# Gated linear attention and a SoLU feed-forward block: every operation in a new written order

## The chip, the cores and the metric

The kernel runs on one core of one Trainium2 chip. The metric is the device time of one execution in microseconds (us), as a median of several runs. The core has five engines with a queue each: TensorE (PE in the profile; PEld are its weight loads), VectorE (DVE), ScalarE (ACT), GpSimd (POOL) and SyncE (SP), which here only issues DMAs. Each queue is worked off in the order in which it is written; an instruction that waits holds up all that stands behind it on its engine.

## What is computed

First a linear attention with a complex decay per key channel (batch 4, 8 heads, 768 steps, head dimension 48), then a feed-forward block over the 3072 rows of 384 numbers:

```python
mag = np.sqrt(a_re * a_re + a_im * a_im)
scale = np.minimum(mag, 0.999) / (mag + 1e-06)
...
for t in range(S):
    new_re = ar * S_re - ai * S_im          # ar, ai: a_re, a_im times scale, at step t
    new_im = ar * S_im + ai * S_re
    S_re, S_im = new_re + k_t (outer) v_t, new_im
    y[t] = q_t @ S_re
...
h = x @ w_in                                # 384 -> 1024, x: y of all heads side by side
solu = h * softmax(h)
ln = (solu - mean) / sqrt(var + 1e-06) * g_ln
out = ln @ w_out                            # 1024 -> 384
```

The weights arrive as 64-bit floats, which no engine computes with; the kernel takes their words apart and puts 32-bit floats together.

## The kernel before

The sequence is cut into six chunks of 128 steps. One unit of work, called a chunk below, is 128 steps of one of the four batch entries with all eight heads: 24 chunks, numbered c = 0 to 23. Two neighbouring chunks are a group (g = 0 to 11) and share their preparation.

*Preparation of a group* (`prep_steps`): from a_re and a_im (tiles `f_ar`, `f_ai`, 128 x 768) the logarithm of the decay and the angle per step. It is a chain of rows of VectorE and ScalarE in turn: clamp (L670, L672), `inverse` (logarithm and exponential), `s1` and `tangent`, `square`, `s2`, `s3`, `s4`. TensorE then sums the logarithms over the steps of the chunk with a triangular matrix (`totals`, tile `f_L`, L713) and the angles likewise (`phases`, tile `f_phase`, L766). Exponentials of the sums give `f_ar` and `f_ai` anew (`decay`), sines give the tile `f_cs` (`trig`). ScalarE needs one function table for exponentials and one for sines; `to_trig` and `to_exp` load them. From one chunk of a batch entry to the next the angle is carried on (`on`, L756) and so is the decay at the last step (`ends`, `tots`); both pass through a small DMA.

*Turning* (`doubled`, `turn`): k and q are scaled by the decay (`decayed`, L727), multiplied by cosine and sine (L794, tiles `f_k2`, `f_q2`, printed as `f_k` and `f_q` in the profile), and transposed by TensorE in halves of four heads (L806, `f_turned`); ScalarE copies the result out of PSUM to `f_kT` and `f_qT`.

*Attention of a chunk* (`chunk_steps`): scores (L827, tile `f_score`) and their mask (L829), the values (L843, L846, tile `f_y`) and their copy `f_xn` (L849), and the carried state (L858, `f_d`). V is also loaded a second time with its rows in reversed blocks (`f_vr`, eight small DMAs a group).

*Feed-forward of a chunk* (`ffn_steps`): transpose of x (`f_xt`, L876), up projection in two halves (`f_h`, L884), exponential and product (L892, L893, tile `f_z`), transposes of z (`f_zt`, L901) and their copies (L902), the mean and variance (`norm`, L914 and on), down projection in two halves (`f_o`, L926), and the scaling by the row's norm `f_rs` with the store (L931, L933).

*Weights* (`weight_steps`): 14 pieces, 6 of w_in and 8 of w_out. A piece is fetched to one of six `f_raw` buffers, two rows of ScalarE (`raised`, L626, L628) and three of VectorE (`convert`, L634, L636, L638) make floats of it. The eight `mean` matmuls (L650) and eight `centre` rows (L655) take the mean out of w_out, so that the layer norm's mean need not be subtracted later. From the fifth chunk on all pieces are fetched once more and inspected (L641).

The PSUM banks: two buffers `f_ps_t` that all transposes and sums take in turn, one bank for each half of the scores, one shared by values and state, two for `f_h`, one for `f_o` (which `f_mean` uses before).

The order of the rows of TensorE, VectorE and ScalarE is the order of the calls in `whole`: a written list for chunks 0 and 1, then a loop over n = 2 to 25 whose body does chunk n's attention, chunk n-1's up projection and chunk n-2's down projection with pieces of the preparation of the next groups, the even n one share, the odd n another. The rows of SP and GpSimd are put in order by the framework's scheduler. Several calls issue rows on two or three engines at once, such as `phases` with six rows on three engines.

## Time and profile before

| | |
|---|---|
| median of 3 runs | 547.28 us (545.79 to 548.36) |
| profiled execution: time, span | 545.41 us, 543.6 us |
| TensorE busy | 472.0 us, 87% |
| VectorE busy | 368.1 us, 68% |
| ScalarE busy | 305.7 us, 56% |
| moved by DMA | 44.7 MB |

The span runs from the first to the last instruction. A row of the 40 slices gives an engine's busy share in tenths for each fortieth of the span, 13.6 us. In the views of waits a row reads: who waited, `<-` for whom, us in total, how often, the longest. In the views of groups a row ends with busy us and the mean ns of one, then the idle time ahead of these rows and who ended it. In the timeline a row begins with its start and its duration in us; in brackets stands the idle time of its engine before it. A matmul of 32-bit floats is two instructions, so that x6 in the profile are three matmuls of the code.

### The profile page before, as it was taken

Reading aid. Unit: us, or ns where it says so; the run is one execution under the profiler, and the core shown is the slowest. Engines: PE = TensorE matmul, PEld = TensorE weight load, DVE = VectorE, ACT = ScalarE, POOL = GpSimd, SP = SyncE. Lnnn points to the kernel's source line nnn. Section 1 sums busy time; section 2 is a strip of 40 time slices with the busy share of each in tenths; the row PEclk is TensorE's granted clock in tenths of the full one; section 3 lists DMA queues with packets and bytes.
Section 4 is the critical chain, followed back from the end, with each engine's and each line's share of the span. In section 5 each row is a group of like instructions: output and inputs, shape, how many; then the busy total and the mean of one; then the engine's idle time right before and its main releaser. Section 6 shows DMA issues by size and latency. Waiting matters only on the chain. (4 is left out here: it accounts for less than half of the span.)

```text
span 543.6 us, 15486 instructions
## 1 busy us (share of the span) xinstructions
PE 472.0 (87%) x6756; PEld 293.1 (54%) x6756; DVE 368.1 (68%) x716; ACT 305.7 (56%) x497; POOL 17.9 (3%) x52
## 2 busy tenths in 40 slices
PE   0264745699999999999999999999999999999994
PEld 0143323455665665666666656556566656666652
DVE  5677435957777867859759669669578677564323
ACT  4766447376666566575575665665656665742220
POOL 0000000000000000000000000000000000000000
PEclk9997786899999999999999999999999999999999
DMA  9895976322624615517317305316223000000001
GB/s 210 203 245 115 183 116 191 102 57 58 120 60 69 139 45 89 119 46 128 80 47 146 60 24 110 60 32 119 45 56 80 16 3 17 16 16 2 16 16 36
DMA packets 148076, 44.74 MB, mean 82 GB/s; under 512 B 141216, under 2 KB 144288, under 8 KB 148000
## 3 DMA queue, kind: packets, MB, share of 16 engines
q1 hardware_dynamic: 147152, 43.28, 37.6%
q8 instruction: 55, 0.90, 0.7%
q10 hardware_dynamic: 848, 0.40, 0.3%
q14 instruction: 21, 0.17, 0.1%
HBM read 38.87 MB, written 4.72 MB: 80 GB/s over the span
## 5 line engine op out<-in xcount | busy, mean ns | idle before, releaser
L884 PE MATMUL f_h<-f_w_in,f_xT 128*128 128x512 f32 x288 | 135.3, 607 | 8.5 <-ACT f_xT L879 8.5
L926 PE MATMUL f_o<-f_w_out,f_zT 128*128 128x384 f32 x384 | 133.5, 492 | 2.9 <-DVE f_w_out L655 2.9
L926 PEld LDWEIGHTS f_o<-f_w_out,f_zT 128*128 128x128 f32 x384 | 70.3, 192 | 43.4 <-DVE f_w_out L655 3.1
L884 PEld LDWEIGHTS f_h<-f_w_in,f_xT 128*128 128x128 f32 x288 | 51.8, 192 | 58.5 <-issue 48.0
L892 ACT ACTIVATE f_z<-f_h 128x512 f32<-128x512 f32 x48 | 28.7, 597 | 87.9 <-PE f_h L884 87.7
L893 DVE TENSOR_TENSOR f_z<-f_h,f_z 128x512 f32<-128x512 f32 x48 | 33.1, 690 | 44.0 <-ACT f_z L892 44.0
L806 PE MATMUL f_turned<-f_mats,f_k 128*96 128x128 f32 x192 | 32.1, 293 | 17.8 <-DVE f_k L794 17.8
L902 ACT COPY f_zT<-f_zt 128x512 f32<-128x512 f32 x48 | 26.7, 587 | 25.8 <-PE f_zt L901 25.2
L806 PEld LDWEIGHTS f_turned<-f_mats,f_k 128*96 128x96 f32 x192 | 21.8, 132 | 34.8 <-DVE f_k L794 25.4
L849 DVE COPY f_xn<-f_y 128x384 f32<-128x384 f32 x24 | 13.2, 552 | 37.7 <-PE f_y L846 32.3
L808 ACT COPY f_kT<-f_turned 96x512 f32<-96x512 f32 x48 | 27.7, 576 | 18.4 <-PE f_turned L806 18.4
L713 PE MATMUL f_L<-f_lr,f_mats 128*128 128x384 f32 x48 | 19.0, 522 | 18.5 <-DVE f_lr L706 18.5
L806 PE MATMUL f_turned<-f_mats,f_q 128*96 128x128 f32 x192 | 31.1, 288 | 2.7 <-DVE f_q L794 2.7
L827 PEld LDWEIGHTS f_score<-f_qT,f_kT 96*32 96x32 f32 x1536 | 28.8, 110 | 8.0 <-issue 8.0
L829 DVE TENSOR_TENSOR f_att<-f_score,f_mats 128x512 f32<-128x512 f32 x48 | 30.8, 683 | 2.5 <-PE f_score L827 2.5
L827 PE MATMUL f_score<-f_qT,f_kT 96*32 96x96 f32 (+3 forms) x1536 | 32.0, 235 | 0.0
L714 DVE TENSOR_SCALAR f_lr<-f_L 128x384 f32<-128x384 f32 x24 | 13.3, 557 | 25.8 <-PE f_L L713 25.0
L914 DVE BATCH_NORM_STATS2 f_bs<-f_z 128x6 f32<-128x512 f32 x48 | 30.7, 681 | 0.0
L846 PE MATMUL f_y<-f_state,f_qT 96*32 96x48 f32 x1280 | 30.1, 205 | 0.0
L808 ACT COPY f_qT<-f_turned 96x512 f32<-96x512 f32 x48 | 28.1, 586 | 2.7 <-PE f_turned L806 1.5
L901 PEld LDWEIGHTS f_zt<-f_mats,f_z 128*128 128x128 f32 x192 | 21.5, 141 | 13.2 <-DVE f_lr L714 8.5
L901 PE MATMUL f_zt<-f_mats,f_z 128*128 128x128 f32 x192 | 27.9, 279 | 0.2
(101 smaller groups left out, 751.7 us busy)
## 6 DMA issues: line engine op xcount, KB each, us to landing
f_raw<-in_moe_w_in_dram SPq DMA_DIRECT2D x12, 512.0 KB, 5.7
f_raw<-in_moe_w_out_dram SPq DMA_DIRECT2D x16, 384.0 KB, 4.2
f_ar<-in_a_re_dram SPq DMA_DIRECT2D x24, 192.0 KB, 3.8
f_ai<-in_a_im_dram SPq DMA_DIRECT2D x24, 192.0 KB, 4.1
f_q<-in_q_dram SPq DMA_DIRECT2D x24, 192.0 KB, 4.3
f_k<-in_k_dram SPq DMA_DIRECT2D x24, 192.0 KB, 4.1
f_v<-in_v_dram SPq DMA_DIRECT2D x24, 192.0 KB, 4.8
out_dram<-f_ot SPq DMA_DIRECT2D x24, 192.0 KB, 1.9
```

Source lines behind the costliest of these rows:

```text
L806: nc.tensor.transpose(out=ps[0:D2, i], in_=T[nm + "2", c][:, half * 4 + i].rearrange("p u d -> p (u d)"), identity=ident)
L808: nc.scalar.copy(out=T[nm + "T", c][:, half * 512:half * 512 + 512], in_=ps[0:D2].rearrange("p i t -> p (i t)"))
L827: nc.tensor.matmul(out=ps[r0:r0 + 32, i, r:], lhsT=KT[:, x * P + r:x * P + r + 32], rhs=QT[:, x * P + r:(x + 1) * P], start=True, stop=True)
L829: nc.vector.tensor_tensor(out=st["att"][:, half * 4:half * 4 + 4].rearrange("p (i u) t -> p i u t", u=2), in0=ps.rearrange("p (i u) t -> p ...
L846: nc.tensor.matmul(out=y[r:r + 32, hs], lhsT=T["qT", c][:, x * P + r:x * P + r + 32], rhs=state[b][:, hs], start=False, stop=True)
L884: nc.tensor.matmul(out=h, lhsT=st["xT"][:, c * P:(c + 1) * P], rhs=w_in[:, c, half * 512:(half + 1) * 512], start=(c == 0), stop=(c == KD ...
L892: nc.scalar.activation(out=z, in_=h, func=AF.Exp, accum_out=sums[:, ti * B + b, half:half + 1])
L893: nc.vector.tensor_tensor(out=z, in0=h, in1=z, op=OP.mult)
L901: nc.tensor.transpose(out=ps[:, i * P:(i + 1) * P], in_=st["z"][:, c * P:(c + 1) * P], identity=ident)
L902: nc.scalar.copy(out=st["zT"][:, half * 512:(half + 1) * 512], in_=ps)
L914: nc.vector.bn_stats(out=bs[:, i], in_=z[:, i * 512:(i + 1) * 512])
L926: nc.tensor.matmul(out=st["o"], lhsT=st["zT"][:, c * P:(c + 1) * P], rhs=w_out[:, c], start=(c == 0), stop=(c == KF - 1))
```

## The change

Every call is split so that it issues rows on one engine only: `phases` becomes `phase0`, `phase1`, `nearest0`, `nearest1`, `part0`, `part1`; `score` leaves its mask to `mask`; `turn` leaves its copy to `turned`; and so on. The steps are kept in a table by name and number, and three lists of words give the order: START for the first chunks, 190 steps one by one, and EVEN and ODD for the loop, which together are one pair of chunk periods. In a word such as `kt1:2` stand the step and the chunk; in EVEN and ODD the number is added to n, and with a g it is added to the group's number. The scheduler no longer orders SP and GpSimd: their rows too come in the order of the lists. Besides, the scaling by `f_rs` moves from VectorE to ScalarE, the two small DMAs from ScalarE's queue to SP's, the verdict's rows (a check over all chunks) go to the very end, and the fetches for the inspection are at other places.

```diff
+START = """
+load_ar:0 load_ai:0 fetch:0 fetch:1 fetch:4 fetch:3 clamp:0 inverse:0 fetch:2 ratio:0 raised:0 load_ar:1
...
+EVEN = """
+turn_x:-1 solu1:-2 score0:0 zt1:-2 down0:-2 clamp:g1 load_k:g1 inverse:g1 turned_x:-1 kt1:0 ks1:g0 zT1:-2 add:-1
...
+ODD = """
+inspect:-9 qt0:1 qT0:1 zT0:-1 down1:-2 load_ar:g2 exp1:-1 scale:-2 store:-2
...
-            nc.scalar.dma_start(out=st["ends"], in_=up[P - 1:P, :])
+            nc.sync.dma_start(out=st["ends"], in_=st["ar"][P - 1:P, :])
...
-                nc.scalar.activation(out=t, in_=ps, func=AF.Identity, bias=magic)
-                nc.vector.scalar_tensor_tensor(out=t, in0=t, scalar=MAGIC, in1=ps, op0=OP.subtract, op1=OP.subtract)
+        def nearest(i):
+            nc.scalar.activation(out=st["f"][:, i * DM:(i + 1) * DM], in_=st["phase", i], func=AF.Identity, bias=magic)
...
-            nc.vector.tensor_scalar(out=o, in0=st["o"], scalar1=st["rs"], scalar2=None, op0=OP.mult)
+        def scale():
+            st["out"] = ffp.tile([P, DM], FP, tag="ot", name="f_ot")
+            nc.scalar.activation(out=st["out"], in_=st["o"], func=AF.Copy, scale=st["rs"])
...
+    for s in START.split():
+        nm, i = s.split(":")
+        go(nm, int(i))
+    for n in range(2, NC * B + 2):
+        for s in (ODD if n % 2 else EVEN).split():
+            nm, i = s.split(":")
+            go(nm, n // GB + int(i[1:]) if i[0] == "g" else n + int(i))
+    go("verdict", 0)
...
-        inner.enter_context(tc.manual_schedule(engines={mybir.EngineType.Activation, mybir.EngineType.PE, mybir.EngineType.DVE}))
+        inner.enter_context(tc.manual_schedule(engines={mybir.EngineType.Activation, mybir.EngineType.PE, mybir.EngineType.DVE,
+                                                    mybir.EngineType.SP, mybir.EngineType.Pool}))
```

Three places show what that does to the queues. The first is the start of SP's queue, the loads of the opening. Before:

```order
L592 DMA f_ai<-in_a_im_dram 128x8x48 x2
L619 DMA f_raw<-in_moe_w_in_dram 128x1024 x2
L592 DMA f_q<-in_q_dram 128x8x48 x2
L592 DMA f_k<-in_k_dram 128x8x48 x2
L619 DMA f_raw<-in_moe_w_in_dram 128x1024 x4
L592 DMA f_v<-in_v_dram 128x8x48 x2
L601 DMA f_vr<-in_v_dram 32x4x48 x8
L592 DMA f_ar<-in_a_re_dram 128x8x48 x2
L592 DMA f_ai<-in_a_im_dram 128x8x48 x2
L987 DMA f_g_ln<-in_moe_g_ln_dram 128x8x1
L619 DMA f_raw<-in_moe_w_out_dram 128x768 x5
```

and now, with `f_ends` the decay's last step, which waits for ScalarE:

```order
L626 DMA f_ai<-in_a_im_dram 128x8x48 x2
L657 DMA f_raw<-in_moe_w_in_dram 128x1024 x5
L626 DMA f_ar<-in_a_re_dram 128x8x48 x2
L626 DMA f_q<-in_q_dram 128x8x48 x2
L657 DMA f_raw<-in_moe_w_in_dram 128x1024
L626 DMA f_ai<-in_a_im_dram 128x8x48 x2
L767 DMA f_ends<-f_ar 16x1x48
L657 DMA f_raw<-in_moe_w_out_dram 128x768
L626 DMA f_k<-in_k_dram 128x8x48 x2
L657 DMA f_raw<-in_moe_w_out_dram 128x768
L826 DMA f_on<-f_f 1x16x48
L626 DMA f_v<-in_v_dram 128x8x48 x2
```

The weights of w_in and the second group's a_re have moved ahead of the first group's k and v, and the two small DMAs stand between the loads. The second place is VectorE's queue at the end of the second group's preparation, from the last row of its phases to the doubled k and q of chunk 2. Before:

```order
L769 TENSOR_SCALAR f_cs_650<-f_f_651 128x8x48
L634 TENSOR_SCALAR f_w_out_121<-f_raw_314 128x384
L636 SCALAR_TENSOR_TENSOR f_w_out_121<-f_raw_314,f_w_out_121 128x384
L638 ISA f_w_out_121<-f_w_out_121,f_bits_671 128x768
L727 TENSOR_TENSOR f_k_325<-f_k_325,f_ai_182 128x384
L727 TENSOR_TENSOR f_q_322<-f_q_322,f_ar_179 128x384
L794 TENSOR_TENSOR f_k2_679<-f_cs_650,f_k_325 128x768
L794 TENSOR_TENSOR f_q2_681<-f_cs_650,f_q_322 128x768
```

and now:

```order
L814 TENSOR_SCALAR f_cs_582<-f_f_583 128x8x48
L672 TENSOR_SCALAR f_w_out_121<-f_raw_343 128x384
L674 SCALAR_TENSOR_TENSOR f_w_out_121<-f_raw_343,f_w_out_121 128x384
L676 ISA f_w_out_121<-f_w_out_121,f_bits_571 128x768
L921 COPY f_xn_653<-f_y_614 128x384
L672 TENSOR_SCALAR f_w_out_121<-f_raw_547 128x384
L674 SCALAR_TENSOR_TENSOR f_w_out_121<-f_raw_547,f_w_out_121 128x384
L676 ISA f_w_out_121<-f_w_out_121,f_bits_589 128x768
L771 TENSOR_TENSOR f_q_489<-f_q_489,f_ar_171 128x384
L854 TENSOR_TENSOR f_q2_674<-f_cs_582,f_q_489 128x768
L771 TENSOR_TENSOR f_k_471<-f_k_471,f_ai_200 128x384
L854 TENSOR_TENSOR f_k2_689<-f_cs_582,f_k_471 128x768
```

Before, three pieces of weights are converted behind this stretch and one in it; now the last two stand in it and none behind. The third place is VectorE's queue in the loop around the angle that is carried on (L756 before, L796 now). Before:

```order
L714 TENSOR_SCALAR f_lr_751<-f_L_973 128x384
L714 TENSOR_SCALAR f_lr_751<-f_L_976 128x384
L756 SCALAR_TENSOR_TENSOR f_x0_752<-f_on_259,f_x0_752 1x768
L931 TENSOR_SCALAR f_ot_980<-f_o_841,f_rs_913 128x384
L768 SCALAR_TENSOR_TENSOR f_f_997<-f_f_997,f_phase_998 128x384
```

and now:

```order
L757 TENSOR_SCALAR f_lr_781<-f_L_933 128x384
L757 TENSOR_SCALAR f_lr_781<-f_L_939 128x384
L796 SCALAR_TENSOR_TENSOR f_x0_782<-f_on_275,f_x0_782 1x768
L899 TENSOR_TENSOR f_att_941<-f_score0_130,f_mats_118 128x512
L899 TENSOR_TENSOR f_att_941<-f_score1_131,f_mats_118 128x512
L812 SCALAR_TENSOR_TENSOR f_f_991<-f_f_991,f_phase_992 128x384
```

The scaling of the output has left VectorE, and the masks of the pair's second chunk stand between the carried angle and the phases.

More of the change, by code (lines that the diff above doesn't have):

```diff
@@ L2 @@
 from contextlib import ExitStack
+from functools import partial
 import numpy as np
@@ new lines, in prep_steps @@
+        own = dict(clamp=clamp, inverse=inverse, ratio=ratio, tangent=tangent, square=square, secant=secant,
+                   fourth=fourth, size=size, eps=eps, lnm=lnm, grow=grow, decay=decay, ends=ends, trig=to_trig,
+                   angle=angle, cos=cos, sin=sin, exp=to_exp)
+        for i in range(GB):
+            own.update({f"total{i}": partial(total, i), f"low{i}": partial(low, i), f"phase{i}": partial(phase, i),
+                        f"nearest{i}": partial(nearest, i), f"part{i}": partial(part, i),
+                        f"ks{i}": partial(scaled, "k", i), f"qs{i}": partial(scaled, "q", i)})
@@ L959, in verdict @@
                                 op0=OP.not_equal)
-    def run(steps):
-        for f in steps:
-            f()
-    N = NC * B
-    load(0, ("ar", "ai"))
     to_exp()
```

533 lines of the change are left out of this document (189 added, 344 removed).

## The prediction

> **What bounds the kernel now.** I read the page first: engine totals and the 40 slices.
>
> ```profile
> span 543.6 us, 15486 instructions
> PE 472.0 (87%) x6756; PEld 293.1 (54%) x6756; DVE 368.1 (68%) x716; ACT 305.7 (56%) x497; POOL 17.9 (3%) x52
> ...
> PE   0264745699999999999999999999999999999994
> ...
> DVE  5677435957777867859759669669578677564323
> ...
> DMA  9895976322624615517317305316223000000001
> ```
>
> TensorE is full from the ninth slice on (a slice is 13.6 us) and half empty before. So there are two problems: an opening, and a loop that TensorE bounds. The windows put numbers to both. The opening is cut at 102 us, where the first down projection starts, and the fourth row is one pair of chunk periods, 38.2 us.
>
> ```profile
> core 0: us, PE busy (x) PEld busy (x) DVE busy (x) ACT busy (x) POOL busy (x), PEclk, DMA share, GB/s
> 0.00:35.00 35.00, 6.80 (x13) 3.07 (x14) 22.53 (x44) 22.10 (x28) 0.20 (x4) 1.00 0.93 208
> 0.00:102.00 102.00, 43.72 (x523) 26.49 (x523) 62.96 (x125) 58.43 (x85) 0.20 (x4) 0.87 0.83 182
> 102.00:538.15 436.15, 428.32 (x6233) 266.58 (x6233) 305.13 (x593) 247.23 (x412) 17.75 (x48) 1.00 0.29 60
> 188.40:226.60 38.20, 37.68 (x596) 23.59 (x595) 29.42 (x56) 23.42 (x39) 1.48 (x4) 1.00 0.42 87
> ```
>
> In the opening no engine is full: TensorE works 43.7 of 102 us, VectorE 63.0, ScalarE 58.4. Afterwards TensorE stands idle only 436.15 - 428.32 = 7.8 us, 0.5 us a pair. So nearly all that a new order can win lies ahead of 102 us. Next, who waits there. First TensorE, then VectorE, up to 103 us:
>
> ```profile
> PE f_L L713 <- DVE f_lr L706: 18.5, 1, 18.5
> PE f_turned L806 <- DVE f_k L794: 17.5, 3, 10.7
> ...
> DVE f_w_out L638 <- ACT f_bits L628: 13.1, 6, 5.6
> DVE f_f L768 <- ACT f_f L767: 6.2, 3, 5.6
> DVE f_ar L670 <- DMA f_ar<-in_a_re_dram: 3.9, 1, 3.9
> ```
>
> TensorE waits for VectorE's preparation, and VectorE waits in turn for ScalarE in the middle of the weight conversions (13.1 us on L638), with its preparation rows queued behind them. The timeline shows the costliest place (85.76 and 88.19) and others that I use below:
>
> ```profile
> 6.08 0.95 DVE L670 TENSOR_SCALAR_CACHE_REDUCE f_ar<-f_ar 128x768 f32<-128x768 f32 x1 [3.88 <-DMA f_ar<-in_a_re_dram]
> ...
> 40.77 0.84 ACT L675 ACTIVATE f_lr<-f_ar 128x768 f32<-128x768 f32 x1 [2.56 <-DVE f_ar L670]
> ...
> 57.66 4.57 PE L884 MATMUL f_h<-f_w_in,f_xT 128*128 128x512 f32 x6 [8.47 <-ACT f_xT L879]
> 64.37 2.74 PE L884 MATMUL f_h<-f_w_in,f_xT 128*128 128x512 f32 x6
> ...
> 85.76 0.56 DVE L638 CUSTOM_DVE_ANT_0 f_w_out<-f_w_out,f_bits 128x768 uint16<-128x768 uint16 x1 [5.63 <-ACT f_bits L628]
> ...
> 88.19 1.09 PE L806 MATMUL f_turned<-f_mats,f_k 128*96 128x128 f32 x4 [10.72 <-DVE f_k L794]
> ...
> 102.06 4.54 PE L926 MATMUL f_o<-f_w_out,f_zT 128*128 128x384 f32 x8 [2.89 <-DVE f_w_out L655]
> ...
> 115.44 2.75 PE L926 MATMUL f_o<-f_w_out,f_zT 128*128 128x384 f32 x8
> ...
> 500.04 0.60 PE L806 MATMUL f_turned<-f_mats,f_q 128*96 128x128 f32 x4
> 504.03 1.33 PE L827 MATMUL f_score<-f_qT,f_kT 96*32 96x128 f32 x64
> ```
>
> **The opening, part by part.** The first down projection reads all of w_out, so it waits for the eight centring rows (L655), and these for all weight conversions. VectorE's own work up to there is the floor. It had 62.96 us. The new START list moves behind this point the clamp of the third group (0.95 for its first row, 1.6 in all), one of the two scalings of k and of q of the second group (2 x 0.55, below) and its three short rows for the decay's ends (together another 0.55): 59.7 us stay.
>
> ```profile
> L727 DVE TENSOR_TENSOR f_q<-f_q,f_ar 128x384 f32<-128x384 f32 x24 | 13.3, 552 | 0.2 <-ACT f_ar L720 0.2
> ```
>
>  Of them 1.5 us of memsets run before the first load lands at 6.08. If VectorE never waited again it would be done at 6.1 + 58.2 = 64.3, and one turn of z (0.5) later the down projection starts: 64.8.
>
> To this come VectorE's waits. In the first 35 us it idled 35 - 22.53 = 12.5 us, of them 4.6 before the load; the rest, 7.9, is the chain of the first group (logarithm, exponential, tangent, sums over time, sine), in which each row needs the one before. The new order leaves that chain as it is, so I keep 7.9. Behind it I walked the new rows of the three engines with the durations of the trace: ScalarE begins to prepare the second group right after the sines of the first (about 33 us, where the old order has it at 40.8), the two masks wait for scores (1.1), the first attention copy for its values (0.9), and logarithm to decay about 1.3: 3.3 us. The conversions no longer stand in front of rows that are ready. The walk's milestones: the first doubled k ends at 34 us, the first values start at 44, the first up projection at 50, the second group's total sums at 54, its doubled k ends at 68, the last centring row at 74 to 75. Sum: 64.8 + 7.9 + 3.3 = 76.0, against 102.06: **26.1 us less**.
>
> That needs the bytes in time. Loads and weights of START:
>
> ```profile
> f_raw<-in_moe_w_in_dram SPq DMA_DIRECT2D x12, 512.0 KB, 5.7
> f_raw<-in_moe_w_out_dram SPq DMA_DIRECT2D x16, 384.0 KB, 4.2
> f_ar<-in_a_re_dram SPq DMA_DIRECT2D x24, 192.0 KB, 3.8
> ...
> out_dram<-f_ot SPq DMA_DIRECT2D x24, 192.0 KB, 1.9
> ```
>
> Six and eight weight pieces are 6.3 MB, the operands up to the third group about 6 MB, the constants 0.3: 12.5 MB, at the 208 GB/s of the first 35 us 60 us; the last weight piece is the 10.6th MB, 51 us, and ScalarE wants it at about 58. The row of the page that looks worst, the ends and phase DMAs now in SP's queue, stops SP at the decay (about 23 us), when 5.4 MB are asked for and 26 us are needed to bring them; so that wait is covered by the transfers in flight. Were that cover gone, each us of it would delay every weight behind.
>
> Further along TensorE has done a little more at this point than before: one half of the next up projection (2.74) in place of half a q turn (0.60) and half the scores (0.67 of 1.33): 1.3 us, rounded down because neighbours on TensorE overlap. It also arrives busier. Before, the first eight matmuls of the down projection took 4.54 us; warm they take 2.75. I count 1.0 of the 1.8.
>
> **The loop.** TensorE's work, 37.7 us a pair, does not change; only its waits can. From 103 us to the end they are:
>
> ```profile
> PE f_phase L766 <- DVE f_x L756: 2.9, 10, 0.3
> PE f_turned L806 <- DVE f_q L794: 2.4, 10, 0.3
> ```
>
> Both should go: in my walk through the new rows the angle's correction ends 0.9 us before the phase sum is its turn (half the scores and a turn of z now stand between), and the doubled q 1.4 us or more before it is turned. In exchange the whole preparation now runs inside one pair. Its rows, from clamp to the turned q, add up to about 25 us by their durations, and 13 us of the 38.2 are left for others' rows in between; my walk ends with the turned q about 2.4 us before the scores want it, and with the exit of one down projection (0.6 on ScalarE) 0.9 us before the bank is wanted. No wait comes out of it, but margins below 1 us do not always hold: I count 2.5 of the 5.3 us. The scaling of the output by f_rs leaves VectorE for ScalarE:
>
> ```profile
> L879 ACT COPY f_xT<-f_xt 128x384 f32<-128x384 f32 x24 | 11.5, 478 | 24.1 <-PE f_xt L876 23.9
> L931 DVE TENSOR_SCALAR f_ot<-f_o,f_rs 128x384 f32<-128x384 f32 x24 | 14.6, 607 | 9.8 <-PE f_o L926 6.4 <-PEq L1231 3.4
> ```
>
> Between 0.48 and 0.61 us each on an engine that is busy 23.4 of 38.2: nothing. V and its reversed copy are now loaded in the pair that uses them:
>
> ```profile
> 167.24 4.58 SPq L601 DMA_DIRECT2D f_vr<-in_v_dram  x8
> ...
> 174.92 3.18 SPq L592 DMA_DIRECT2D f_v<-in_v_dram  x2
> ```
>
> These ten DMAs take 7.8 us to issue; with k's two ahead and the landing behind they need about 12, and are read 16 us into the pair: hidden, with 4 us to spare. Weights fetched again for inspection, and the order on GpSimd, have more room than that: nothing.
>
> **The end.** The last z is turned and copied in four steps, then the verdict's matmul comes, then the last down projection:
>
> ```profile
> 529.74 1.04 PE L901 MATMUL f_zt<-f_mats,f_z 128*128 128x128 f32 x8
> 530.43 1.07 ACT L902 COPY f_zT<-f_zt 128x512 f32<-128x512 f32 x2 [2.38 <-PE f_zt L901]
> ...
> 532.02 5.43 PE L926 MATMUL f_o<-f_w_out,f_zT 128*128 128x384 f32 x16
> ...
> 537.54 0.62 DVE L931 TENSOR_SCALAR f_ot<-f_o,f_rs 128x384 f32<-128x384 f32 x1 [3.44 <-PEq L1231]
> ```
>
> The down projection's first half now needs only the first copy, 1.4 instead of 2.3 us after the turn's start: 0.9 less. The verdict runs after it; its five short rows (under 1 us) lie beside the last store, which takes 1.9 us to land and closes the span.
>
> **Sum.** 26.1 + 1.3 + 1.0 + 2.5 + 0.9 = 31.8 us. The profiled execution took 545.41 us (span 543.6 and 1.8 around it): 513.6. The median of the three runs, 547.28, is 1.9 above it; from there **515.5 us**.
>
> **Rivals.**
> *TensorE bounds the opening at half clock.* At 57.66, after 8.5 us of idling, six matmuls took 4.57 us; at 64.37 the same took 2.74. If it stays slow all through START, the three half up projections cost 3 x 1.83 = 5.5 more and, at the same ratio of 1.67, the means and sums beside them about as much again; I put half of these 11 us on the path to the centring: 5 us, 520.5. For it: the bursts of the transposes are still apart. Against: from the first up projection on, TensorE has rows without gaps of over 2 us in my walk. The Trainium skill, "TensorE: Matmul & The Clock Gate" (Part 1: The HAM clock gate), says that the array runs at half its clock until it has been busy for a window of about 3.4 us, and falls back after an idle one. By that rule the stretch up to 50 us is slow and the rest is not, which the two rows above agree with; it is what I assumed.
>
> *The transfers bound the opening.* At the 182 GB/s of the whole opening the 10.6th MB lands at 58 us and not 51, and if SP stands at a wait with little in flight, at 65; the last conversions and means then come 4 to 9 us late: 520 to 525. For it: the DMA slices fall to 3 and 2 wherever SP was held.
>
> *The opening reaches its floor.* If most of the 11 us of waits fill up, 68 instead of 76: 507.5. Against: the first chain has nothing else to run beside it until weights land.
>
> *The loop gets a new wait, and the kernel is slower.* Preparation inside one pair makes a circle: clamp, chain, turns, scores, next clamp. If the handovers of its 25 rows and the others' rows in between make it longer than the pair, every one of 10.5 pairs pays. The walk leaves 2.4 us; the gain of 29.3 outside the loop is lost once a pair is 2.8 longer, so the chain must run 5.2 us later than walked. At 6.2 later the time is 547.28 - 29.3 + 10.5 x 3.8 = 558. Against: VectorE has 28.2 and ScalarE 24.6 of 38.2 us to do, so both catch up. A milder form, 0.5 us a pair, gives 523.
>
> **How the numbers follow.** The forecast (511 to 519) gets 0.50, the half clock 0.14, the transfers 0.14, the floor 0.09, the mild loop wait 0.08, the long one 0.05. The range 507 to 526 leaves out the long loop wait and the outer ends of the floor and the transfers. Differences under 0.5% (2.7 us), about what a measurement of this kernel can tell from none, need a loss of 29 us in the opening or the loop: 0.01. Slower is 0.04 of the long wait; faster 0.95.
>
> **What would show it.** The first matmul of f_o starts near 76 us; VectorE's waits on the conversions (13.1) nearly vanish; the slices of TensorE reach 9 in the seventh. A pair takes 37.8 to 38.2 us, without a wait of TensorE above 0.5. If the first f_o comes after 82, look whether the conversions wait for DMA or the means run slow. If a pair is longer than 38.7, the circle is the cause and the forecast is wrong.

## The result and the profile after

The changed kernel took 506.58 us (median of 4 runs, 505.10 to 508.81), against 547.82 us of the kernel before in the same session: a ratio of 0.926, with a 95% interval of 0.921 to 0.930. The forecast was 515.5, so the gain was 41 us where 32 had been worked out; the time lies 0.4 us below the range (507 to 526), less than the four runs differ, and at the number of the rival "The opening reaches its floor" (507.5). The profiled execution took 505.1 us, the fastest of the four; its span is 40.3 us shorter than that of before. A ratio compares the undisturbed executions of both kernels, which are all of them but for one kernel below, where five of ten were in a slower state.

The page of the changed kernel, engine totals and slices (12.6 us each):

```profile
span 503.3 us, 15535 instructions
...
PE 463.2 (92%) x6756; PEld 294.1 (58%) x6756; DVE 358.3 (71%) x692; ACT 314.9 (63%) x521; POOL 18.0 (4%) x52
...
PE   0258998999999999999999999999999999999994
...
DVE  5899999586677687687687687687687687672331
```

TensorE is full from the fifth slice on, but for an 8 in the seventh (forecast: the seventh, before: the ninth), and VectorE at 9 from the third to the seventh, where it had stood at 7, 7, 4, 3 and 5. The windows of the same kernel, cut where the prediction's were (70.44 us is the first down projection):

```profile
core 0: us, PE busy (x) PEld busy (x) DVE busy (x) ACT busy (x) POOL busy (x), PEclk, DMA share, GB/s
0.00:35.00 35.00, 6.78 (x13) 3.13 (x14) 26.40 (x55) 25.76 (x34) 0.20 (x4) 1.00 0.88 202
0.00:70.44 70.44, 39.18 (x494) 23.61 (x495) 60.06 (x116) 54.07 (x80) 0.20 (x4) 1.00 0.87 190
188.40:226.60 38.20, 38.20 (x601) 24.62 (x600) 28.92 (x55) 24.82 (x42) 1.48 (x4) 1.00 0.42 97
```

The opening ends at 70.4 us instead of 102.1. Its granted clock (PEclk) reads 1.00, where it was 0.87. That figure needs care: in this trace the first record of the clock begins at 38.3 us (37.3 in before), and the view prints 1.00 where there is none. The rows show that TensorE ran at half rate until then, in both kernels: the same sums took 2.93 us for the first group and 1.45 for the second.

```profile
18.82 2.93 PE L754 MATMUL f_L<-f_lr,f_mats 128*128 128x384 f32 x4 [18.82 <-DVE f_lr L749]
...
51.00 1.45 PE L754 MATMUL f_L<-f_lr,f_mats 128*128 128x384 f32 x4
```

The waits of TensorE in the opening, all that it has from 80 us to the end, and the longest of VectorE's up to 71 us:

```profile
PE f_L L754 <- DVE f_lr L749: 18.8, 1, 18.8
PE f_turned L864 <- DVE f_k L854: 4.8, 1, 4.8
PE f_phase L805 <- ACT f_x L791: 4.4, 1, 4.4
...
PE f_o L1008 <- ACT f_zT L984: 0.4, 1, 0.4
PE f_L L754 <- DVE f_tot L788: 0.3, 1, 0.3
PE f_turned L864 <- ACT f_kT L868: 0.2, 1, 0.2
...
DVE f_ar L712 <- DMA f_ar<-in_a_re_dram: 3.9, 1, 3.9
DVE f_ai L714 <- DMA f_ai<-in_a_im_dram: 1.0, 1, 1.0
...
DVE f_lr L757 <- PE f_L L754: 0.7, 1, 0.7
```

What is left in the opening is the first chain (18.8, 4.4 and 4.8 us); the wait of 10.72 for the second group's doubled k is gone, and so is VectorE's wait on the conversions (13.1). In the loop TensorE has two single waits left, 0.3 and 0.2 us; the f_o wait is that of the very end.

Four points in the two traces divide the 40.3 us. Up to the first matmul of f_o: 102.06 to 70.4, **31.7**. From there to the first phase sum of the loop (19.01 to 17.57): **1.4**. Nine pairs, from that phase sum to the last one (348.28 to 342.22; a pair 38.8 and then 38.1): **6.1**. From the last phase sum to the end of the span (74.25 to 73.11): **1.1**.

And within the opening: the first turned k, the end of the first chain, starts at 34.1 us before and at 34.33 after. All of the 31.7 us lies behind it: from the first turned k to the first f_o it was 68.0 us and is 36.0.

### The profile page after: what moved, and what is told of

Its sections match the earlier page's. It is cut to its first block, busy times and chain, and to the rows that moved or that the text cites. A ratio compares the mean times of both kernels' runs of the same rounds, so it can differ in the third digit from the quotient of the medians.

```text
span 503.3 us, 15535 instructions
## 1 busy us (share of the span) xinstructions
PE 463.2 (92%) x6756; PEld 294.1 (58%) x6756; DVE 358.3 (71%) x692; ACT 314.9 (63%) x521; POOL 18.0 (4%) x52
## 3 DMA queue, kind: packets, MB, share of 16 engines
q1 hardware_dynamic: 147856, 43.34, 38.8%
## 4 chain that ended last, share of the span: by engine, by line
PE 83%; DVE 7%; ACT 4%; DMA 2%; SPq 2%; issue 1%; ACTq 0%
PE f_o L1008 24%; PE f_h L961 23%; PE f_turned L864 8%; PE f_score L895 6%; PE f_zt L981 4%; PE f_phase L805 4%; PE f_L L754 4%; PE f_y L913 4%; PE f_d L929 3%; PE f_y L916 3%; SPq L626 2%; PE f_xt L952 1%; DMA f_raw<-in_moe_w_in_dram 1%; DMA f_v<-in_v_dram 1%; DVE f_k L854 1%
## 5 line engine op out<-in xcount | busy, mean ns | idle before, releaser
L961 PE MATMUL f_h<-f_w_in,f_xT 128*128 128x512 f32 x288 | 129.3, 597 | 0.0
L973 DVE TENSOR_TENSOR f_z<-f_h,f_z 128x512 f32<-128x512 f32 x48 | 32.0, 686 | 39.6 <-ACT f_z L968 39.6
L868 ACT COPY f_qT<-f_turned 96x512 f32<-96x512 f32 x48 | 26.8, 582 | 30.6 <-PE f_turned L864 30.6
L754 PE MATMUL f_L<-f_lr,f_mats 128*128 128x384 f32 x48 | 19.9, 540 | 19.1 <-DVE f_lr L749 18.8
L895 PEld LDWEIGHTS f_score<-f_qT,f_kT 96*32 96x32 f32 x1536 | 30.6, 110 | 11.7 <-issue 11.3
L895 PE MATMUL f_score<-f_qT,f_kT 96*32 96x128 f32 (+3 forms) x1536 | 37.1, 236 | 0.0
L899 DVE TENSOR_TENSOR f_att<-f_score,f_mats 128x512 f32<-128x512 f32 x48 | 32.7, 682 | 5.8 <-PE f_score L895 5.8
L864 PE MATMUL f_turned<-f_mats,f_k 128*96 128x128 f32 x192 | 30.4, 283 | 5.1 <-DVE f_k L854 4.8
L864 PE MATMUL f_turned<-f_mats,f_q 128*96 128x128 f32 x192 | 28.1, 282 | 1.9 <-ACT f_ar L732 0.8
L916 PEld LDWEIGHTS f_y<-f_state,f_qT 96*32 96x32 f32 x1280 | 27.7, 110 | 0.0
L864 PEld LDWEIGHTS f_turned<-f_mats,f_q 128*96 128x96 f32 x192 | 21.2, 129 | 10.5 <-issue 5.4
```

Source lines behind the costliest of these rows:

```text
L754: nc.tensor.matmul(out=ps, lhsT=tri, rhs=st["lr"][:, i * DM:(i + 1) * DM], start=True, stop=True)
L864: nc.tensor.transpose(out=ps[0:D2, j], in_=T[nm + "2", c][:, half * 4 + j].rearrange("p u d -> p (u d)"), identity=ident)
L868: nc.scalar.copy(out=T[nm + "T", c][:, half * 512:half * 512 + 512], in_=st[nm, half][0:D2].rearrange("p i t -> p (i t)"))
L895: nc.tensor.matmul(out=ps[r0:r0 + 32, i, r:], lhsT=KT[:, x * P + r:x * P + r + 32], rhs=QT[:, x * P + r:(x + 1) * P], start=True, stop=True)
L899: nc.vector.tensor_tensor(out=st["att"][:, half * 4:half * 4 + 4].rearrange("p (i u) t -> p i u t", u=2), in0=scores[half].rearrange("p (i ...
L916: nc.tensor.matmul(out=y[r:r + 32, hs], lhsT=T["qT", c][:, x * P + r:x * P + r + 32], rhs=state[b][:, hs], start=False, stop=True)
```

## The experiments

Twelve kernels ran. Where profiles are compared in the opening, the distance from the first turned k to the first f_o is taken: the first turned k itself comes between 34.3 and 36.3 us in profiles of kernels whose first chain is untouched, since the first transfers do not land at the same time in every execution.

**Opening and loop apart.** First the old opening with the new loop. START holds before's order of loads and steps, and a few words to hand over; the two small DMAs of the first groups are on ScalarE's queue again:

```diff
-load_ar:0 load_ai:0 fetch:0 fetch:1 fetch:4 fetch:3 clamp:0 inverse:0 fetch:2 ratio:0 raised:0 load_ar:1
...
+load_ar:0 load_ai:0 fetch:0 fetch:1 load_q:0 load_k:0 fetch:2 fetch:3 fetch:4 fetch:5 load_v:0 load_vr:0
+load_ar:1 load_ai:1 gain:0 clamp:0 inverse:0 raised:0 ratio:0 tangent:0 square:0 secant:0 convert:0 raised:1
...
```

> START is replaced by the old opening, step for step in the old order, with the old order of loads (and the two small DMAs of the first two groups on ScalarE's queue as before), then the eight steps that START has beyond it; EVEN and ODD stay. If opening and loop simply add (31.6 of the 40.3 us of span lie ahead of the first down projection, 8.7 behind it): f_o starts near 102 to 107 us and the kernel takes about 539 to 542 us. If the old opening's waits come from the loads of the third and fourth group and the refetched weights that the scheduler put in front, f_o starts near 90 and the time is about 527.

Measured: 538.93 us, ratio 0.983 (0.980 to 0.987). The loop alone is worth 8.5 to 9 us by the medians. Its trace shows the new loop's pace behind the old opening: nine pairs take 342.1 us, 38.1 a pair, as in the changed kernel (342.22). But its first f_o comes at 108.2 us, past the expected 107 and 6.1 later than in before, and from there to the end it takes 430.6 us, 2.3 less than the changed kernel. So the rebuilt opening is not before's to the last us, and why it is slower stays open.

Then the reverse: the new opening, and the loop in before's order of words (with VectorE scaling the output rows).

```diff
-turn_x:-1 solu1:-2 score0:0 zt1:-2 down0:-2 clamp:g1 load_k:g1 inverse:g1 turned_x:-1 kt1:0 ks1:g0 zT1:-2 add:-1
...
+load_k:g1 load_q:g1 load_v:g1 load_vr:g1 load_ar:g2 load_ai:g2 again:-4 score0:0 mask0:0 score1:0 mask1:0
...
-            nc.scalar.activation(out=st["out"], in_=st["o"], func=AF.Copy, scale=st["rs"])
+            nc.vector.tensor_scalar(out=st["out"], in0=st["o"], scalar1=st["rs"], scalar2=None, op0=OP.mult)
```

> START stays, then the old loop's order (masks, copies and scaling where they stood, scaling on VectorE, small DMAs on ScalarE's queue), with the steps between the two openings in one short list. If opening and loop add: f_o starts near 71 to 73 us, a pair of chunk periods is 38.8 us instead of 38.1, and the time is 513 to 516. If the new loop's gain is a property of the steady order alone, TensorE again waits 0.2 to 0.3 us for the carried angle and for the doubled q once a pair; if not, these waits do not come back.

Measured: 560.84 us, ratio 1.024 (1.020 to 1.027), 45 us off. Its own trace shows a fault of the experiment. Timeline of SP's queue around one pair and its wait there, the row of VectorE that waits there, and TensorE's largest wait in the loop:

```profile
161.37 0.34 SPq L1019 DMA_DIRECT2D out_dram<-f_ot  x1
161.76 1.18 SPq L627 DMA_DIRECT2D f_k<-in_k_dram  x2
...
164.74 5.82 SPq L638 DMA_DIRECT2D f_vr<-in_v_dram  x8
...
173.35 1.56 SPq L658 DMA_DIRECT2D f_raw<-in_moe_w_in_dram  x1
...
SPq L1019 <- DVE f_ot L1014: 27.9, 2, 20.5
...
178.31 0.69 DVE L680 TENSOR_REDUCE f_least<-f_raw 128x1 f32<-128x512 f32 x1 [4.58 <-DMA f_raw<-in_moe_w_in_dram]
...
PE f_zt L982 <- DVE f_lr L758: 32.7, 7, 5.5
```

In before's order of words the loads stand behind a store. With SP in written order the store waits 20.5 us for its rows, and all loads behind it wait too; the weights to be inspected land late, VectorE stands at the inspection with `low` behind it, and TensorE stands at z's transposes for the PSUM bank that `low` would free. Before left the order of SP to the scheduler. So the same kernel ran with SP and GpSimd ordered by the scheduler again:

```diff
-        inner.enter_context(tc.manual_schedule(engines={mybir.EngineType.Activation, mybir.EngineType.PE, mybir.EngineType.DVE,
-                                                    mybir.EngineType.SP, mybir.EngineType.Pool}))
+        inner.enter_context(tc.manual_schedule(engines={mybir.EngineType.Activation, mybir.EngineType.PE, mybir.EngineType.DVE}))
```

> The new opening and the old loop's order of words again (with VectorE scaling the output rows and the small transfers on ScalarE's queue, as in before), but SP's and GpSimd's queues ordered by the framework's scheduler, as they were in before. In the run with the old loop (560.84 us) SP's queue in a written order held the weight rows to be looked at again and the next group's loads behind a store of output rows that was not ready: VectorE waited 47.1 us for f_raw in it. Theory A (the two parts of the change add up, and only SP's queue spoiled that run): opening gain 31.6 and the loop back at 441.5 us, so 507 + 8.7 = 513 to 517 us, with no wait of VectorE for f_raw above 3 us and pairs of 38.6 to 38.9 us. Theory B (the old loop's order of VectorE and TensorE itself does not fit behind the new opening): 530 us or more, with TensorE's wait for f_lr (32.7 us there) still above 15 us.

Measured: 517.45 us, ratio 0.946 (0.942 to 0.950), half a us above theory A's range. From the first f_o to the end of the span it takes 441.2 us, before's 441.5, a pair 38.8, and its waits of TensorE in the loop are before's two (of the first row 0.8 us lie in the opening, the other ten waits are 0.2 to 0.3 each):

```profile
PE f_turned L865 <- DVE f_q L855: 3.2, 11, 0.8
PE f_phase L806 <- DVE f_x L797: 2.9, 10, 0.3
```

So the two halves add up to 39 of the 41 us: the new opening alone takes off about 30, the new loop alone 8.5 to 9. That the loop's part is 11 us when counted from this kernel is the opening's other end: its first f_o is 38.5 us behind the first turned k and not 36. The old loop wants more steps done ahead of it, which a list of 15 words behind START does here.

**SP's and GpSimd's order by itself.** The same edit made to the changed kernel:

> The lists stay, but SP's and GpSimd's rows are ordered by the scheduler again (one line). Theory: they matter little, since no engine waits for a DMA for more than 1.4 us in the new kernel: 505 to 509, pair 38.1. Rival: the scheduler puts transfers ahead that collide with V's loads in the pair that needs them, and TensorE waits at the values: a pair longer by 0.5 or more, 512 and more.

Measured: 506.78 us, ratio 0.926 (0.922 to 0.929). Nothing. In the opening the scheduler keeps the words' order of loads almost as it is, so this run tests the order in the loop: there the written order is no gain, and in the run above it was a trap.

**The order of the loads.** Only the words of the loads in START stand in before's order (operands of the first group first, weights later); all other words stay.

> Only SP's rows of START are changed: the old order of loads (k and q of the first group before four weight pieces, V and its reversed copy before the second group's a_re); the rows of the other engines stay. If the order of the compute rows makes the opening: f_o within 2 us of 70.4, time 506 to 509. If the order of the loads carries it: the conversions of w_in and the second group wait, f_o at 76 or later, 512 and more.

Measured: 516.51 us, ratio 0.943 (0.940 to 0.946). Ten of the 41 us are lost when the loads do not fit the words. The window of its first chain, to be held against the 26.40 and 25.76 above, and VectorE's longest wait there behind the first loads:

```profile
0.00:35.00 35.00, 5.86 (x8) 2.35 (x8) 20.31 (x41) 21.64 (x29) 0.20 (x4) 1.00 0.94 214
...
DVE f_w_in L672 <- DMA f_raw<-in_moe_w_in_dram: 2.6, 1, 2.6
```

VectorE did 6.1 us less in it. Not because fewer bytes came (214 GB/s against 202): the weights that conversions need were behind the operands that nobody wanted yet. The conversions had no data in the first chain's gaps and held up the rows behind them: ScalarE waited 3.6 us for a weight piece and began the decay at 25.8 us instead of 22.4. First turned k at 40.9, first f_o at 80.7, and from there 433.2 us to the end, as in the changed kernel (432.9). In before, with these loads and the old words, the first turned k came at 34.1. The new loads under the old words were not run, so the ten us are the price of a mismatch and not the worth of the loads by themselves.

**Which engine bounds the opening?** Behind the first turned k VectorE is busy 34.32 of 36.1 us and TensorE 33.03 (row below). Four kernels took work away there: seven of eight centring rows of VectorE (behind the second group's doubled q), six of eight mean products of TensorE, both, and one row of VectorE in each conversion of w_out (ahead of that doubled q).

```diff
-            nc.vector.scalar_tensor_tensor(out=w_out[:, c], in0=w_out[:, c], scalar=g_ln[:, c:c + 1], in1=T["mean"],
-                                           op0=OP.mult, op1=OP.subtract)
+            if c == 0:
+                nc.vector.scalar_tensor_tensor(out=w_out[:, c], in0=w_out[:, c], scalar=g_ln[:, c:c + 1], in1=T["mean"],
+                                               op0=OP.mult, op1=OP.subtract)
...
-            nc.tensor.matmul(out=T["mean"], lhsT=T["gs"][:, c:c + 1].to_broadcast([P, P]), rhs=w_out[:, c],
-                             start=(c == 0), stop=(c == KF - 1))
+            if c in (0, KF - 1):
+                nc.tensor.matmul(out=T["mean"], lhsT=T["gs"][:, c:c + 1].to_broadcast([P, P]), rhs=w_out[:, c],
+                                 start=(c == 0), stop=(c == KF - 1))
...
-            nc.vector.scalar_tensor_tensor(out=x, in0=hi, scalar=-2 ** 30, in1=x, op0=OP.bitwise_and,
-                                           op1=OP.bitwise_or)
+            if w is w_in:
+                nc.vector.scalar_tensor_tensor(out=x, in0=hi, scalar=-2 ** 30, in1=x, op0=OP.bitwise_and,
+                                               op1=OP.bitwise_or)
```

> Seven of the eight centring rows of w_out left out (part of the computation is left out): VectorE has 4.2 us less to do just ahead of the opening's last activation. Theory VectorE (it alone bounds the opening): first f_o at 66.1 us instead of 70.4, time 502.3 us. Theory both (VectorE and TensorE are both full after the first chain, 33.66 and 32.40 of 35.44 us): TensorE has its own rows until 69.5, so first f_o at 69.4 to 70.0, time 505.5 to 506.6 us.

> Six of the eight products that sum the mean of w_out left out (part of the computation is left out): TensorE has 6 x 0.81 = 4.9 us less to do in the opening. Theory VectorE alone or both: VectorE's rows end where they ended, first f_o at 70.0 to 70.4 us, time 506 to 506.6 us. Theory TensorE alone (it bounds the opening from 34 us on): first f_o at 65.5 to 66.5 us, time 502 us.

> Both left out (part of the computation is left out): seven centring rows and six mean products. Theory both: only now does the opening get shorter, first f_o at 65.8 to 67 us and time 502 to 503 us, more than the two single cuts together. Theory VectorE alone: the same as with the seven centring rows alone. Theory TensorE alone: the same as with the six products alone.

> The middle one of the three VectorE rows of each conversion of w_out left out (part of the computation is left out): 8 x 0.56 = 4.5 us less for VectorE between 37 and 61 us, ahead of the second group's doubled q and not behind it, as the centring rows were. Read from first turned k to first f_o, which is free of when the first transfers land. Theory VectorE (after the first chain the opening is VectorE's row of work up to the doubled q, and then TensorE's): 36.1 us (after) becomes 33.0 to 33.6, where TensorE's own 33.0 us of work stops it, and the time 503.3 to 504.3 us. Theory chain (the second group's handovers between VectorE, ScalarE and TensorE set it, not the amount of work): 35.3 to 36.1 us and 506 to 506.8 us.

| left out | us of work | median us | first turned k to first f_o |
|---|---|---|---|
| nothing (changed kernel) | | 506.58 | 36.0 |
| centring rows | VectorE 4.2 | 505.02 | 35.4 |
| mean products | TensorE 4.9 | 506.52 | 38.4 |
| both | 4.2 and 4.9 | 506.18 | 36.4 |
| conversion rows | VectorE 4.5 | 507.70 | 36.9 |

No cut shortened the opening by the work it took out. "VectorE alone" and "TensorE alone" fall by the first two runs (the second with a slow clock, below); the third should have given 502 to 503 us by "both", and did not. The last run bears on the choice between amount and chain for VectorE; the windows from first turned k to first f_o, changed kernel and then the run without the conversion rows, and VectorE's longest wait in the latter:

```profile
34.30:70.40 36.10, 33.03 (x485) 21.08 (x486) 34.32 (x63) 28.97 (x48) 0.00 (x0) 1.00 0.85 177
...
36.25:73.19 36.94, 33.13 (x485) 21.74 (x485) 30.28 (x55) 29.03 (x48) 0.00 (x0) 1.00 0.87 173
...
DVE f_q L772 <- ACT f_ar L766: 1.7, 1, 1.7
```

VectorE's 4.5 us of work became waits: for ScalarE's decay (1.70), for TensorE's sums (1.16) and scores (0.57, 0.59), and for logarithms (0.63, 0.45). So the amount of VectorE's work does not set the second group's speed. The 36.9 us are 0.8 more than the chain theory allowed, too, and TensorE shows why. Two of its rows in the changed kernel, then the same two here:

```profile
38.70 0.77 PE L895 MATMUL f_score<-f_qT,f_kT 96*32 96x128 f32 x32
46.48 0.66 PE L929 MATMUL f_d<-f_v,f_k 128*32 128x48 f32 x32 [1.62 <-issue]
...
40.79 1.30 PE L896 MATMUL f_score<-f_qT,f_kT 96*32 96x128 f32 x32
49.76 0.66 PE L930 MATMUL f_d<-f_v,f_k 128*32 128x48 f32 x32 [2.41 <-issue]
```

The full clock came 5.8 us behind the first turned k (record from 42.07 us) instead of 4.0, and a stop at issue lasted 0.8 us longer, so the first up projection began 14.7 us behind the first turned k instead of 13.3. Without these 1.4 us 35.6 would be left, an estimate, which lies in the chain theory's range and not in VectorE's (33.0 to 33.6).

What does set the speed is not settled. In the changed kernel ScalarE is busy almost without a gap from 43.00 us to the decay that the doubled q needs:

```profile
43.00:61.30 18.30, 16.51 (x204) 9.24 (x193) 16.76 (x35) 17.83 (x27) 0.00 (x0) 1.00 0.89 182
```

None of the four kernels took work from ScalarE. That ScalarE's own rows bound this stretch fits all of them as well as handovers between three queues do, and VectorE's scaling of q, the row ahead of the doubled q, waits for that decay in all four (0.52 us in three, 1.70 in the last). A kernel with less for ScalarE there would tell.

The run without the mean products got slower in that stretch by 2.3 us, and the clock tells why:

```profile
60.00:65.00 5.00, 2.42 (x8) 1.25 (x9) 4.34 (x9) 4.35 (x7) 0.00 (x0) 0.77 0.68 129
65.00:70.00 5.00, 5.00 (x58) 3.23 (x57) 5.00 (x10) 1.65 (x4) 0.00 (x0) 0.54 1.13 199
...
67.67 3.69 PE L962 MATMUL f_h<-f_w_in,f_xT 128*128 128x512 f32 x6
```

Where the products are missing TensorE waits (1.31 and 0.90 us), the granted clock falls at 62.7 us for 6.8 us, and the up projection takes 3.69 instead of 2.84 us. The mean products are work that also keeps the clock up. At half clock these 6.8 us can have cost 3.4 at the most, which leaves 35.0 us, an estimate, and not the 31 to 32 of "TensorE alone". The run with both cuts fell into the same hole, with 0.95 over 35 to 70 us, that is 3.4 us at half clock and at most 1.7 us of work: 34.7 are left, and not the 31.5 to 32.7 of "both". A run at full clock is missing, so for "both" this is argued and not shown.

**The verdict.** The branch after it depends on its result; in the changed kernel it stands behind the last output products. The word went back ahead of the last two.

```diff
     for n in range(2, NC * B + 2):
+        if n == NC * B + 1:
+            go("verdict", 0)
...
-    go("verdict", 0)
```

> The verdict (the rows that decide whether the general kernel has to run) ahead of the last two output products, as in before, instead of behind them; all else as in after. Theory (the verdict at the end is paid: the first f_o of the last two to the end of the span took 12.4 us in after and 11.6 in before, and a branch on TensorE's queue took 4.4 us behind the last work): 0.6 to 1.0 us less, 505.6 to 506.0. Rival (the verdict is hidden beside the last rows, as the prediction had it): 506.4 to 506.8.

Measured: 507.08 us, ratio 0.927 (0.924 to 0.931): the same as the changed kernel within the runs, above both ranges. In the changed kernel the last scaling starts 6.8 us ahead of the span's end, in this one 6.1, as in before. But now the verdict's product stands between the two halves of the last down projection:

```profile
495.14 0.19 PE L1045 MATMUL f_count<-f_row,f_mats 128*1 128x3 f32 x2
495.26 2.85 PE L1008 MATMUL f_o<-f_w_out,f_zT 128*128 128x384 f32 x8
```

From their start (492.37) to their end these take 5.7 us instead of 5.4. From the start of the last f_o to the end of the span it is 12.0 us instead of 12.4, less than the runs can tell.

**A first chain with less in its way.** With the verdict early, the second weight piece's rows behind the square and its logarithm, and both scalings of k ahead of the sixth conversion.

```diff
-tangent:0 raised:1 square:0 convert:1 secant:0 load_q:0 size:0 fourth:0 eps:0 fetch:5 convert:0 raised:4 lnm:0
+tangent:0 square:0 secant:0 raised:1 load_q:0 size:0 convert:1 fourth:0 eps:0 fetch:5 convert:0 raised:4 lnm:0
...
-load_k:0 raised:6 fetch:12 convert:5 ks0:0 cos:0 turn_ends:0 sin:0 exp:0 load_v:0 ks1:0 k2:0 kt1:0 tot:0 kt0:0
...
+load_k:0 raised:6 fetch:12 ks0:0 ks1:0 cos:0 turn_ends:0 sin:0 exp:0 load_v:0 k2:0 kt1:0 tot:0 kt0:0
+inverse:1 q2:0 kT1:0 convert:5 gain:0 qt1:0 kT0:0 qt0:0 load_vr:0 fetch:8 q2:1 k2:1 qT1:0 convert:6 qT0:0 ratio:1 kt0:1
...
```

> The verdict early, and in the first chain three conversion steps moved off the way: the second weight piece's ScalarE rows behind the square and its logarithm (they held it 0.65 us), its VectorE rows behind the size, and both scalings of k ahead of the sixth conversion (it held the doubled k 0.9 us). Theory (the opening is the first chain and then a full TensorE and VectorE, so what the first chain saves the whole kernel saves): 0.8 + 0.65 + 0.87 = 2.3 us less, 504.0 to 504.8, first turned k at 32.8 us instead of 34.33 with the first loads landing alike. Rival (the conversions only come later and VectorE, full until 61 us, gives it back): the verdict's 0.8 alone, 505.6 to 506.0.

Measured: 508.07 us, ratio 0.928 (0.925 to 0.931): 1.5 us above the changed kernel's median (runs of 507.19 to 508.95 against 505.10 to 508.81), on the rival's side and beyond it. VectorE now idles 1.88 us where the moved conversion had run, and then has two conversions between the size (14.24) and the next row of the chain, which starts at 18.81 instead of 17.81. The first turned k comes at 34.47, no earlier, and from there it is 39.5 us instead of 36.0 to the first f_o. The sixth conversion now stands between the two halves of the doubled q (1.8 us of VectorE from 35.28): a conversion that is taken out of a gap of the first chain comes back in the second. The full clock came late as well, 5.8 us behind the first turned k instead of 4.0; how the 3.5 us divide stays open.

**What a wait in the loop costs.** From the fourth group on the Square row is repeated six times (5.3 us more by the trace).

```diff
-            nc.scalar.activation(out=st["ar"], in_=st["x0"], func=AF.Square)
+            for _ in range(7 if g > 2 else 1):
+                nc.scalar.activation(out=st["ar"], in_=st["x0"], func=AF.Square)
```

> From the fourth group on the Square row of the preparation is done seven times instead of once, which puts 6 x 0.83 = 5.0 us into the chain of every pair's preparation (nine pairs) and into ScalarE's queue, with the same values. Prediction's walk (2.4 us of slack from clamp to the doubled q): TensorE waits 2.6 us in each of nine pairs, 506.6 + 23 = 530 us, with waits for f_q or f_phase in the loop. Rival (the chain has over 5 us of slack, since VectorE and ScalarE stand idle a third of the pair): 506.5 to 508 us, TensorE full in the loop.

Measured: 549.29 us (median of ten, 541.20 to 552.07), ratio 0.998 (0.993 to 1.002). All of the gain is gone; both theories missed. From the first f_o to the end it took 473.8 us, 40.9 more. TensorE's waits in the loop, one of them in the timeline with the rows that cause it, and the windows around:

```profile
PE f_turned L865 <- ACT f_qT L869: 26.5, 9, 3.0
...
199.99 6.10 ACT L733 ACTIVATE f_ar<-f_x 128x768 f32<-128x768 f32 x7 [0.90 <-DVE f_x L729]
...
207.53 1.05 ACT L869 COPY f_qT<-f_turned 96x512 f32<-96x512 f32 x2
...
208.15 1.09 PE L865 MATMUL f_turned<-f_mats,f_k 128*96 128x128 f32 x4 [3.00 <-ACT f_qT L869]
209.03 3.66 PE L1009 MATMUL f_o<-f_w_out,f_zT 128*128 128x384 f32 x8
...
206.00:208.00 2.00, 0.00 (x0) 0.00 (x0) 0.91 (x2) 1.97 (x5) 0.00 (x0) 0.86 0.00 0
208.00:210.00 2.00, 1.85 (x6) 1.52 (x7) 1.76 (x8) 1.89 (x6) 0.08 (x1) 0.50 0.04 8
210.00:212.00 2.00, 2.00 (x6) 1.03 (x6) 2.00 (x6) 1.63 (x2) 0.66 (x2) 0.78 0.00 0
```

It is not the chain that TensorE waits for. The copies of the turned q stand behind the Square rows in ScalarE's queue, and TensorE waits for the PSUM bank that they free. The slack at that place was 5.3 - 3.0 = 2.3 us. That this is near the 2.4 us of the prediction's walk is chance, since the walk meant the chain, whose margin stays untested. But a wait of 2.94 us (26.5 in nine) cost 40.9 / 9 = 4.5: after it the clock stands at half, the next turn takes 1.09 instead of 0.60 and the down projection 3.66 instead of 2.75. By the three windows the half clock lasts 0.56 + 2.0 + 0.88 = 3.4 us, which is 1.7 us of work; with the wait that makes 4.6.

## Why the prediction was right, and where its sizes were off

The mechanism held: most of the gain is in the opening, VectorE's conversions no longer stand before rows that are ready, the loop keeps its 24 chunks at TensorE's pace, and none of the rivals that make the kernel slower came. The number was not met: 511 to 519, which had 0.50, lies above the measured 506.58. That this is the floor rival's 507.5 (0.09) is half luck: of the 8 us that the rival wanted from the opening 5.6 came, and the rest is the loop's, from which it expected nothing more. Step by step:

- **The opening, 26.1 forecast, 31.7 measured.** The floor was right in size (VectorE's work to the first f_o 60.06 us, 59.7 forecast). The failed term is the waits: 7.9 in the first chain and 3.3 behind it. VectorE idled 35 - 26.40 = 8.6 us in the first 35, of them 4.9 before the first load and 3.7 behind it instead of 7.9, and 1.8 in the rest instead of 3.3. (The prediction took 1.5 us for the rows before the load, where a window shows 1.24: 7.9 was 7.6, the floor 0.3 more, and the sum the same.) "The new order leaves that chain as it is, so I keep 7.9" was half true: the chain's length stayed (34.1 to 34.33), but more fits into its gaps. The new load order brings w_in early enough for all six of its conversions (before: five, 1.8 us each) and the second group's a_re early enough for its clamp (1.6 us); VectorE got 26.40 us done there instead of 22.53. The milestones show it come in: doubled k 34.3 (forecast 34), first values 41.7 (44), first up projection 47.7 (50), second group's sums 51.0 (54), its doubled k 64.4 (68), last centring row 69.2 (74 to 75).
- **The floor as a reason.** VectorE's work was taken as what bounds the opening. The cuts say no: neither 4.2 nor 4.5 us less of it ends the opening earlier by more than 0.6. That the number came out near is luck as far as the runs show; ScalarE, which the floor left out, is the fuller engine ahead of the doubled q (17.83 of 18.30 us).
- **The loads**, costed at nothing as long as the bytes arrive in time, lose ten of the 41 us where their order does not fit the words. The sum of bytes was the wrong question; which bytes come first was the right one. The rival of the transfers did not happen: behind the first loads VectorE has one wait of 0.5 us that the view puts down to a load, and it ends with ScalarE's decay (60.46 to 61.30), which the same row waits for in eight other kernels here. SP's wait for the decay (18.3 to 23.2 us) was not covered by transfers in flight as worked out: from 22 to 24 us the DMA share is 0.14. It cost nothing because no engine wanted those bytes yet.
- **The half clock** as a rival did not happen either: it lasted to 38.3 us and not to 50, the clock is full from there to 499 us, and the first up projection takes 2.84 us. The Trainium skill, "TensorE: Matmul & The Clock Gate" (Part 1: The HAM clock gate), gives the half rate and a window of about 3.4 us; the 3.4 us at 0.50 behind a wait agree. It has the clock fall after an idle window; here it fell after about 2.3 us of a wait, and in the run without mean products behind waits of 1.31 and 0.90 us.
- **TensorE further along, and warm: 2.3 forecast, 1.4 measured** to the first phase sum of the loop.
- **The loop, 2.5 forecast, 6.1 measured.** The two waits did go; halving the 5.3 us for margins below 1 us was the error, since no wait came in their place. The other 0.8 is between TensorE's rows, where this trace shows no wait. The pair of before had been taken for 38.2 us, the length of a window; its phase sums (at 121.07, 159.83, 198.75 us and on) show 38.8.
- **The loop waits as rivals** were priced too low per us: a wait of 2.94 us cost half as much again as it lasted. The loss of 2.8 us a pair that eats the gain comes with a wait of 1.8 us, if that rate holds for shorter waits, which no run shows.
- **Scaling on ScalarE, V's late loads, GpSimd's order: nothing**, and no wait on them appears; they were not run one by one. SP's order in the loop: nothing as well, by its own run.
- **The end, 0.9 forecast, 1.1 measured.** The first half of the down projection starts 1.45 us after the turn of z instead of 2.28. The verdict, "beside the last store", costs 0.7 behind the last scaling; ahead of it, it costs 0.3 on TensorE.

## What to carry to other kernels

Look at a slow opening as a set of dependent chains that share in-order queues: put what can wait (here weight conversions) into the first chain's gaps, and order the loads so that it has its data there. Test "engine X bounds this stretch" by leaving out some of X's work before optimizing it: a stretch can be 95% busy on one engine and still be held by something else. Where TensorE bounds a loop, count a wait of about 3 us in it at one and a half times its length, and where a store and loads share a queue, never let the store stand ahead of its data with loads behind it.

## What the hardware showed beyond that

Less work can take longer: without six mean products (4.9 us of TensorE) the stretch behind the first chain took 2.3 us more, since the clock fell (0.77 and 0.54 in two windows). A wait of 2.94 us was followed by 3.4 us at half clock. And the first transfers land at other times in other executions: the first turned k, with an untouched first chain, started at 34.3 to 36.3 us, which is as much as the effects sought in the last experiments.

When the clock falls can be read from the fourteen traces of this case. The recorded clock changes only on a grid of 3.41 us. In the two cases above TensorE was busy 1.10 us (204.05 to 207.46) and 1.20 us (59.33 to 62.74) of the grid step ahead of the fall, so it is the busy share of the step that goes with it and not the length of one wait. Over all steps at full clock, all 47 with a share under 45% were followed by half clock and none of the 1857 with 53% and more; the six between went both ways. From half clock it came back after all 32 steps with 83% and more, and after none of the 18 under 79%.
